# Bfloat16 partition sums and float32r parts for two batches of attention scores

## The chip, the cores and the metric

The kernel runs on one core of one Trainium2 chip. A core has a matrix engine (TensorE, PE in the profile), a vector engine (VectorE, DVE), a scalar engine (ScalarE, ACT), a general engine (GpSimd, POOL) and a queue engine that issues the transfers (SyncE, SP). The metric is the device time of one execution in microseconds.

## The reference, cut to what matters

Attention with a threshold on the scores, then an MLP with a residual (the "moe" part), then a mixing block (the "moe2" part). Four batches, eight heads, 576 tokens, 64 columns a head, 512 columns in all.

```python
scores = scale * np.matmul(q, k.transpose(0, 1, 3, 2))
thresh = np.max(scores, axis=-1, keepdims=True) - tau
scores = np.where(scores >= thresh, scores, -1000000000.0)
attn = np.exp(scores - np.max(scores, axis=-1, keepdims=True))
x = np.matmul(attn / (np.sum(attn, axis=-1, keepdims=True) + 1e-09), v)
...
xn = (x - mu) / np.sqrt(var + 1e-06) * g_ln
x = x + np.maximum(xn @ w_ch1, 0.0) @ w_ch2
...
theta = x @ w_theta
u = x + w_tok_r @ (x * np.cos(theta)) + w_tok_i @ (x * np.sin(theta))
out = u + np.maximum(u @ w_ch, 0.0)
```

## The kernel before

The program is written out by a planner (class Plan, lines 118 to 271). Each step of the work is an op with a function that issues its instructions, the ops that it depends on, the buffer places that it takes and gives back (Slot and Res), and an estimated cost on each engine that may run it. The planner plays these costs through eight times and then issues the instructions of every engine in the order of the best play. On the chip each engine works its list in that fixed order and waits where something isn't ready. PE's ops run in the order of a key: attention first, the MLP behind it. Where the play leaves PE without work for over 200 ns, `keep` (line 456) puts small filler matmuls.

Attention goes by couples: `couple(b, t, hp)` is one tile of 128 queries for two heads (pair hp) of batch b. There are four full tiles and one tail tile a batch (64 queries, the two heads stacked in one unit of 128 rows), and four pairs, so 16 full and 4 tail couples for each batch. `Keys` loads the transposed keys of a pair (tile kf, 128 x 576, line 753) and prepares its values; `Queries` loads one tile of queries for all four pairs (qf, line 855). `qk` (line 880) multiplies them in float32: two halves of 288 columns for each unit, where the two heads of a full couple stand on different rows of the array. `unit` then works on each unit: `top` (line 988, DVE) evicts and finds the maximum, `mask` and `expo` follow on ACT, `hi16` and `lo16` split P into two float16 parts (tile ringP), and a transposing DMA writes P's transposes (tile PT, line 1057; NPT places of the resource rPT). Batch 0 (WHOLE) uses transposes on PE instead, with PT as a float32 tile. `pv` (line 918) multiplies P and V into rows of x, for which it needs a free row tile (rXs, eight places). Nine row tiles serve two batches.

When three row tiles are complete, `ln_group` normalises them (tiles xn, resource rN, two places; the weight conversion `cvt` takes its tile a from the same two), makes the transposed operand ringX, and runs part A of the MLP: 12 of 16 chunks with `mlp1` (line 709, p_A) and `mlp2` (line 732, chA). There are six such groups. In groups (1,0) and (1,1) (LNQ) the transposition goes by DMA from a float16 tile x16 (resource rX16, two places); the others transpose on PE (line 1196). After attention, part B runs the other four chunks (p_B and c), then the mixing block follows (th, y, o).

Weights are loaded as raw words (tiles raw, resource rR, four places) and converted to two float16 parts. `group4` (line 566) converts four pieces with one common scale; for it, squares are summed over the partitions by a float32 matmul of one column with a matrix of ones (m5, line 607). It runs 13 times (eight for the MLP's weights, three for wtok, one each for wth and wch). `Keys.total` (line 796) does the same for the values of a pair in batches 1 to 3, 12 times, and `scales` (line 1492) for x, with nine such matmuls, twice. `one16` is a bfloat16 matrix of ones that the filler matmuls use already.

Of the kernel before, what the change touches and what calls it, by code (L numbers as in the profile page):

```python
# [22 lines left out]
KB = 4  # L23
# [9 lines left out]
NP16 = 4  # L33
NPT = 6
NRAW = 4
# [45 lines left out]
BUSY = 0.7  # L81
LATE = 25000.0
PVW = (2, 3)
XQ = (0, 1, 2)
# [190 lines left out]
def tile_kernel(  # L275
# [19 lines left out]
    def f(ap):  # L295
        return ap.bitcast(F32)

    def copy(e, out, in_):
        if e is A:
            A.activation(out=out, in_=in_, func=AF.Copy)  # L300
        elif e is V:
            V.tensor_copy(out=out, in_=in_)
        else:
            G.tensor_scalar(out=out, in0=in_, scalar1=1.0, scalar2=0.0, op0=ALU.mult, op1=ALU.add)  # L304
# [52 lines left out]
    rN = Res("xn", 2)  # L357
    rX16 = Res("x16", NX16)
    rG = Res("g", 8)
# [206 lines left out]
    def group4(name, pieces, acq, start, prev, kind, base, i, by_g, early=False):  # L566
# [38 lines left out]
        def m5(e):  # L605
            st["ps"] = m_tile(ms, [128, 512], f"pw_{name}")
            T.matmul(st["ps"][:, 0:1], lhsT=ones, rhs=st["q"][:, 4:5], start=True, stop=True)

# [132 lines left out]
    class Keys:  # L741


        def __init__(self, b, hp, prev):
# [6 lines left out]
            def load_f(e):  # L751
                k["f"] = ap.tile([128, 576], F32, tag=str(self.sk), name="kf_" + nm)
                Q.dma_start(k["f"], kT[b, hp, :, 0:576])


            self.ready = [op(load_f, prev, (self.sk,), Q=1100, kind=kd)]
            st = self.st = {}
# [38 lines left out]
            def total(e):  # L796
                st["ps"] = m_tile(ms, [128, 512], "pvs_" + nm)
                T.matmul(st["ps"][:, 0:1], lhsT=ones, rhs=st["vm"], start=True, stop=True)

# [43 lines left out]
    class Queries:  # L843


        def __init__(self, b, t, prev):
            nm = f"{b}_{t}"
            kd = "att" if not queries else "prep"
            self.sl = Slot(rQ, 4)
            c0 = 512 if t == TAIL else 128 * (t - 5 if b % 2 else t)  # L850
            q = self.q = {}

            def load_f(e):
                q["f"] = ap.tile([128, 4, 128], F32, tag=str(self.sl), name="qf_" + nm)
                Q.dma_start(q["f"], qT[b, :, :, c0:c0 + 128].rearrange("h p c -> p h c"))

            self.ready = [op(load_f, prev, (self.sl,), Q=1000, kind=kd)]

    def couple(b, t, hp):
# [20 lines left out]
        def qk(ws):  # L880
            def go(e):
                for w in ws:
                    w["S"] = psS.tile([128, 2, 512], F32, tag=str(w["ss"]), name="S_" + w["nm"])
                for n in range(2):
                    for w in ws:
                        r = slice(0, 128) if last else slice(64 * w["j"], 64 * w["j"] + 64)
                        T.matmul(w["S"][:, n, 0:288], lhsT=qd.q["f"][r, hp], rhs=d.k["f"][r, n * 288:(n + 1) * 288],  # L887
                                 start=True, stop=True)
            return go
# [3 lines left out]
        o_qk = qk_last[0] = op(qk(us), d.ready + qd.ready + [qk_last[0]], [w["ss"] for w in us],  # L893
                               (qd.sl,) + ((d.sk,) if final else ()), T=QKT if last else QKC, kind="att", **kw)
        for w in us:
# [221 lines left out]
    def ln_group(p, gi, base):  # L1117
# [44 lines left out]
        for t in range(nt):  # L1162
# [11 lines left out]

            s16 = Slot(rX16)

            def parts(t=t, s16=s16):
                if ("x16", t) not in st:
                    st["x16", t] = ap.tile([128, KB, 2, 128], F16, tag=str(s16), name=f"xn16_{nm}_{t}")
                return st["x16", t]  # L1180
# [311 lines left out]
    def scales(p):  # L1492
        ms, st = Slot(rM), {}

        def m(e):
            st["ps"] = m_tile(ms, [128, 512], f"px_{p}")
            for t in range(9):
                T.matmul(st["ps"][:, 0:1], lhsT=ones, rhs=cst(100 + 9 * p + t), start=(t == 0), stop=(t == 8))

# [18 lines left out]
        kw = dict(kind="ev")  # L1518
        o = op(m, sqs[p], (ms,), T=540, key=-1e6, **kw)
        sx_ops[p] = o = pow2(lambda: st["ps"][:, 0:1], lambda: px(p, X_S), 2.0 ** -30, [o], ms, "ev")  # L1520
# [493 lines left out]
```

## Time and profile before

| what | us |
| --- | --- |
| median of 3 runs | 820.85 (820.68 to 821.62) |
| profiled execution, its own time | 821.73 |
| its span | 819.95 |
| PE busy | 811.4 |
| DVE, ACT, POOL busy | 622.7, 531.7, 371.2 |

The span runs from the first to the last instruction of the profiled execution; the 1.78 us between it and the execution's own time lie outside the program. A row of the timeline gives the start of the first of several equal instructions, the time from there to the end of the last, the engine, the line, the operation with output and inputs, and their number after the x. A float32 matmul shows as two records. A matmul's time includes its way through the pipeline, so the distance from one start to the next says what it holds of the engine.

### The profile page before, as it was taken

The numbers are of one execution on the slowest core, as the hardware profiler recorded it, in microseconds if no ns is written. First come the engines' busy times: TensorE is split into PE (matmuls) and PEld (weight loads), VectorE is DVE, ScalarE is ACT, GpSimd is POOL, SyncE is SP. The second block draws the span as 40 slices with busy tenths as digits, with TensorE's granted clock in tenths as the row PEclk, the third lists the DMA queues.
The fourth block names the chain that finished last, engine by engine and source line by source line (L and its number), as shares of the span: only waits on it lengthen the run. The fifth ranks groups of instructions, "written<-read, shape, count | busy, mean of one in ns | idle before, by whom it ended". The sixth has DMA issues, their size and how long they took to land.

```text
span 819.9 us, 16404 instructions
## 1 busy us (share of the span) xinstructions
PE 811.4 (99%) x6145; PEld 533.8 (65%) x6145; DVE 622.7 (76%) x1291; ACT 531.7 (65%) x966; POOL 371.2 (45%) x462
## 2 busy tenths in 40 slices
PE   9999999999999999999999999999999999999997
PEld 8888866655566666656555555555545777567775
DVE  4879799999688788878757766666667886698843
ACT  4899999998678887887635444455466462474612
POOL 1332478688276468667612212212224470455611
PEclk9999999999999999999999999999999999999999
DMA  8334599996378898996971431663374105010011
GB/s 225 126 108 135 178 217 153 203 200 137 86 144 191 160 215 154 159 195 129 164 227 60 153 130 35 226 224 129 92 166 130 36 16 110 1 60 1 15 44 59
DMA packets 194351, 106.39 MB, mean 130 GB/s; under 512 B 157408, under 2 KB 175328, under 8 KB 194272
## 3 DMA queue, kind: packets, MB, share of 16 engines
q1 hardware_dynamic: 193984, 105.34, 53.7%
q8 instruction: 48, 0.79, 0.4%
q14 instruction: 31, 0.25, 0.1%
q10 hardware_dynamic: 288, 0.00, 0.0%
HBM read 52.50 MB, written 15.73 MB: 83 GB/s over the span
## 4 chain that ended last, share of the span: by engine, by line
PE 95%; ACT 2%; DVE 1%; issue 1%; POOL 0%; DVEq 0%; ACTq 0%; POOLq 0%
PE chA L732 17%; PE p_A L709 17%; PE y L1829 13%; PE S L887 11%; PE p_B L709 6%; PE c L732 6%; PE th L1665 5%; PE pv L902 5%; PE o L1887 4%; PE pv L915 4%; PE tm L965 2%; PE pv L910 2%; PE warm L454 1%; PE th_t L1665 1%; PE ptr L1196 1%
## 5 line engine op out<-in xcount | busy, mean ns | idle before, releaser
L709 PEld LDWEIGHTS <-w 128*128 128x128 f16 x1152 | 110.3, 98 | 80.3 <-issue 7.3
L709 PE MATMUL p_A<-ringX,w 128*128 128x384 f16 x864 | 149.8, 326 | 0.0
L732 PE MATMUL chA<-w,hbuf 128*128 128x512 f16 x648 | 149.4, 379 | 0.0
L732 PEld LDWEIGHTS <-hbuf 128*128 128x128 f16 x864 | 82.3, 99 | 93.7 <-issue 5.4
L994 DVE TENSOR_SCALAR_CACHE_REDUCE ringE<-S,ncoef 128x576 f32<-128x576 f32 x144 | 113.0, 812 | 25.1 <-PE S L887 20.5
L313 POOL TENSOR_TENSOR ringP<-ringE,ringP 128x512 f16<-128x512 f32 (+2 forms) x113 | 110.6, 992 | 18.0 <-ACT ringP L300 14.8
L1010 ACT ACTIVATE ringE<-ringE,tiny 128x576 f32<-128x576 f32 x144 | 105.5, 769 | 2.1 <-POOL tiny L1002 0.4
L887 PE MATMUL S<-kf,qf 64*128 64x288 f32 (+1 forms) x576 | 98.2, 426 | 0.0
L1829 PE MATMUL y<-tok,z 128*128 128x288 f16 x768 | 97.2, 286 | 0.0
L1829 PEld LDWEIGHTS <-z 128*128 128x128 f16 x768 | 75.1, 98 | 19.3
L1036 ACT ACTIVATE ringE<-ringE,ntaup 128x576 f32<-128x576 f32 x108 | 78.4, 764 | 0.1
L715 ACT ACTIVATE hbuf<-p_A 128x384 f16<-128x384 f32 x72 | 35.1, 488 | 57.0 <-PE p_A L709 56.5
L887 PEld LDWEIGHTS S<-kf,qf 64*128 64x128 f32 (+1 forms) x576 | 56.7, 186 | 21.8 <-issue 5.9
L1254 DVE SCALAR_TENSOR_TENSOR x<-chA,qs,x 128x512 f32<-128x512 f32 x54 | 40.3, 748 | 27.3 <-PE chA L732 27.1
L304 POOL TENSOR_SCALAR ringP<-ringE 128x576 f16<-128x576 f32 x59 | 42.6, 725 | 37.0 <-ACT ringE L1036 34.3
L718 DVE SCALAR_TENSOR_TENSOR hbuf<-p_A,hbuf 128x384 f16<-128x384 f32 x72 | 39.5, 550 | 17.1 <-ACT hbuf L715 16.6
L732 PE MATMUL c<-w,hbuf 128*128 128x512 f16 x216 | 50.8, 379 | 0.0
L709 PE MATMUL p_B<-ringX,w 128*128 128x384 f16 x288 | 50.6, 326 | 0.0
L1887 PE MATMUL o<-x1T,cw 128*128 128x288 f16 x384 | 47.7, 286 | 0.0
L313 DVE TENSOR_TENSOR ringP<-ringE,ringP 128x512 f16<-128x512 f32 (+2 forms) x55 | 44.6, 819 | 3.4 <-ACT ringP L300 2.8
L1887 PEld LDWEIGHTS <-cw 128*128 128x128 f16 x384 | 37.6, 98 | 9.7
L308 ACT ACTIVATE x1T<-u,cs 128x576 f16<-128x576 f32 x16 | 12.3, 770 | 47.7 <-DVE u L1856 41.9
(233 smaller groups left out, 1455.0 us busy)
## 6 DMA issues: line engine op xcount, KB each, us to landing
raw_w<-in_w SPq DMA_DIRECT2D x20, 512.0 KB, 4.6
rawe<-in_w SPq DMA_DIRECT2D x12, 512.0 KB, 4.8
raw_tok<-in_wtok SPq DMA_DIRECT2D x12, 432.0 KB, 3.9
qf<-in_qT SPq DMA_DIRECT2D x20, 256.0 KB, 3.3
kf<-in_kT SPq DMA_DIRECT2D x16, 288.0 KB, 3.7
xscr<-x SPq DMA_DIRECT2D x18, 256.0 KB, 2.5
xl<-xscr SPq DMA_DIRECT2D x18, 256.0 KB, 5.1
out<-uo SPq DMA_DIRECT2D x16, 288.0 KB, 2.1
```

What stands on the lines that cost most here:

```text
L304: G.tensor_scalar(out=out, in0=in_, scalar1=1.0, scalar2=0.0, op0=ALU.mult, op1=ALU.add)
L313: e.tensor_tensor(out=out, in0=a, in1=b, op=ALU.subtract)
L709: T.matmul(st["ps"][:, :n], lhsT=ch.w1(a, c), rhs=xt()[:, c, bb, :n], start=(kk == 0), stop=(kk == 11))
L732: T.matmul(ps, lhsT=h[:, a, t * 128:(t + 1) * 128], rhs=ch.w2(bb), start=(first and (a, bb) == M2[0]), stop=(stop and (a, bb) == M2[2]))
L887: T.matmul(w["S"][:, n, 0:288], lhsT=qd.q["f"][r, hp], rhs=d.k["f"][r, n * 288:(n + 1) * 288], start=True, stop=True)
L902: T.matmul(out[:, j * 65:j * 65 + 65], lhsT=(w["pt"] if t < 4 else cp["pt"])[:, c0:c0 + cs.stop - cs.start], rhs=d.st["raw"][:, t, j * 65: ...
L994: V.tensor_scalar(out=st["e"].rearrange("p (a k) -> p a k", a=2), in0=st["S"][:, :, 0:288], scalar1=ncoef, scalar2=None, op0=ALU.mult, op1 ...
L1010: A.activation(out=st["e"], in_=st["e"], func=AF.Prelu, bias=cp["thr"][:, j:j + 1], scale=-1.0, alpha=STEEP)
L1036: A.activation(out=e_of(ws), in_=e_of(ws), func=AF.Exp, bias=ntaup, scale=1.0)
L1665: T.matmul(st["ps"], lhsT=src(a, c), rhs=w[:, c * 512:(c + 1) * 512], start=(kk == 0), stop=(kk == 11))
L1829: T.matmul(st["ps"][n][:, 0:288], lhsT=a, rhs=w[:, n * 288:(n + 1) * 288], start=(k == 0 and q == 0), stop=(k == 8 and q == 2))
L1887: T.matmul(st["ps"][n][:, 0:288], lhsT=w[:, cs], rhs=d["t"][a][:, kk, n * 288:(n + 1) * 288], start=(kk == 0 and q == 0), stop=(kk == 3 an ...
```

## The change

Five edits are made together.

1. The sums over partitions (m5, `total`, and m in `scales`) take the upper 16 bits of the float32 number as bfloat16 and multiply with the bfloat16 ones. In `scales`, a DVE reduction (p0) first adds the nine columns, and one matmul stands for nine.
2. In batches 2 and 3 (those not in QF) keys and queries are loaded into a raw tile of the resource rN, copied to a float32r part hi, and the rest is subtracted into a float32r part lo. `qk` then makes three products in float32r (lo hi, hi lo, hi hi) in place of one in float32. The planner's costs of a couple are 1020 and 850 ns there (1230 and 1000 before).
3. P's transposes have five places in place of six.
4. LN's float16 rows of groups (1,0) and (1,1) take places of rR, those of the raw weights, and the resource rX16 is gone.
5. The constants follow.

```diff
--- before.py
+++ after.py
@@ -31,7 +31,7 @@
 NM = 4
 NE = 4
 NP16 = 4
-NPT = 6
+NPT = 5
 NRAW = 4
 WARM = 20
 WHOLE = ((0, 0), (0, 1), (0, 2), (0, 3))
@@ -80,6 +80,8 @@
 LNQ = ((1, 0), (1, 1))
 BUSY = 0.7
 LATE = 25000.0
+QF = (0, 1)
+QRC, QRT = 1020.0, 850.0
 PVW = (2, 3)
 XQ = (0, 1, 2)
 CX = [0, 760.0, 1250.0]
@@ -295,6 +297,9 @@
     def f(ap):
         return ap.bitcast(F32)
 
+    def top16(ap):
+        return ap.bitcast(BF16)[:, 1:2]
+
     def copy(e, out, in_):
         if e is A:
             A.activation(out=out, in_=in_, func=AF.Copy)
@@ -355,7 +360,6 @@
     rY = Res("y", 0)
     rXs = Res("x", NXS)
     rN = Res("xn", 2)
-    rX16 = Res("x16", NX16)
     rG = Res("g", 8)
     rR = Res("raw", NRAW)
     rQ, rK = Res("q", NQ), Res("k", NK)
@@ -604,7 +608,7 @@
 
         def m5(e):
             st["ps"] = m_tile(ms, [128, 512], f"pw_{name}")
-            T.matmul(st["ps"][:, 0:1], lhsT=ones, rhs=st["q"][:, 4:5], start=True, stop=True)
+            T.matmul(st["ps"][:, 0:1], lhsT=one16[:, 0:128], rhs=top16(st["q"][:, 4:5]), start=True, stop=True)
 
         def m9(e):
             V.tensor_scalar(out=base()[:, 8:12], in0=gsb, scalar1=s_(), scalar2=None, op0=ALU.mult)
@@ -752,8 +756,26 @@
                 k["f"] = ap.tile([128, 576], F32, tag=str(self.sk), name="kf_" + nm)
                 Q.dma_start(k["f"], kT[b, hp, :, 0:576])
 
-
-            self.ready = [op(load_f, prev, (self.sk,), Q=1100, kind=kd)]
+            sraw = Slot(rN)
+
+            def load_k(e):
+                k["raw"] = lp.tile([128, S], F32, tag=str(sraw), name="kraw_" + nm)
+                Q.dma_start(k["raw"], kT[b, hp, :, 0:576])
+
+            def hi_k(e):
+                k["hi"] = ap.tile([128, 576], F32R, tag=str(self.sk), name="khi_" + nm)
+                copy(e, k["hi"], k["raw"])
+
+            def lo_k(e):
+                k["lo"] = ap.tile([128, 576], F32R, tag=f"{self.sk}lo", name="klo_" + nm)
+                sub(e, k["lo"], k["raw"], f(k["hi"]))
+
+            if b in QF:
+                self.ready = [op(load_f, prev, (self.sk,), Q=1100, kind=kd)]
+            else:
+                o = op(load_k, prev, (self.sk, sraw), Q=1100, kind=kd)
+                o = op(hi_k, [o], A=ac(576), V=vc(576, .95), kind=kd)
+                self.ready = [op(lo_k, [o], (), (sraw,), G=gc(576), V=vc(576, 1.4), kind=kd)]
             st = self.st = {}
             src = v[b, hp].rearrange("(j p) c -> p j c", p=128)
             self.sc = None
@@ -795,7 +817,7 @@
 
             def total(e):
                 st["ps"] = m_tile(ms, [128, 512], "pvs_" + nm)
-                T.matmul(st["ps"][:, 0:1], lhsT=ones, rhs=st["vm"], start=True, stop=True)
+                T.matmul(st["ps"][:, 0:1], lhsT=one16[:, 0:128], rhs=top16(st["vm"]), start=True, stop=True)
 
             def s1(e):
                 V.tensor_scalar(out=st["s0"], in0=st["ps"][:, 0:1], scalar1=1.0e-36, scalar2=2.0 ** -28,
@@ -854,7 +876,26 @@
                 q["f"] = ap.tile([128, 4, 128], F32, tag=str(self.sl), name="qf_" + nm)
                 Q.dma_start(q["f"], qT[b, :, :, c0:c0 + 128].rearrange("h p c -> p h c"))
 
-            self.ready = [op(load_f, prev, (self.sl,), Q=1000, kind=kd)]
+            sraw = Slot(rN)
+
+            def load_q(e):
+                q["raw"] = lp.tile([128, S], F32, tag=str(sraw), name="qraw_" + nm)[:, 0:512].rearrange("p (h c) -> p h c", h=4)
+                Q.dma_start(q["raw"], qT[b, :, :, c0:c0 + 128].rearrange("h p c -> p h c"))
+
+            def hi_q(e):
+                q["hi"] = ap.tile([128, 4, 128], F32R, tag=str(self.sl), name="qhi_" + nm)
+                copy(e, q["hi"], q["raw"])
+
+            def lo_q(e):
+                q["lo"] = ap.tile([128, 4, 128], F32R, tag=f"{self.sl}lo", name="qlo_" + nm)
+                sub(e, q["lo"], q["raw"], f(q["hi"]))
+
+            if b in QF:
+                self.ready = [op(load_f, prev, (self.sl,), Q=1000, kind=kd)]
+            else:
+                o = op(load_q, prev, (self.sl, sraw), Q=1000, kind=kd)
+                o = op(hi_q, [o], A=ac(512), V=vc(512, .95), kind=kd)
+                self.ready = [op(lo_q, [o], (), (sraw,), G=gc(512), V=vc(512, 1.4), kind=kd)]
 
     def couple(b, t, hp):
 
@@ -881,17 +922,19 @@
             def go(e):
                 for w in ws:
                     w["S"] = psS.tile([128, 2, 512], F32, tag=str(w["ss"]), name="S_" + w["nm"])
-                for n in range(2):
-                    for w in ws:
-                        r = slice(0, 128) if last else slice(64 * w["j"], 64 * w["j"] + 64)
-                        T.matmul(w["S"][:, n, 0:288], lhsT=qd.q["f"][r, hp], rhs=d.k["f"][r, n * 288:(n + 1) * 288],
-                                 start=True, stop=True)
+                seq = (("f", "f"),) if b in QF else (("lo", "hi"), ("hi", "lo"), ("hi", "hi"))
+                for k, (a, c) in enumerate(seq):
+                    for n in range(2):
+                        for w in ws:
+                            r = slice(0, 128) if last else slice(64 * w["j"], 64 * w["j"] + 64)
+                            T.matmul(w["S"][:, n, 0:288], lhsT=qd.q[a][r, hp], rhs=d.k[c][r, n * 288:(n + 1) * 288],
+                                     start=(k == 0), stop=(k == len(seq) - 1))
             return go
 
         final = t == (8 if odd else TAIL)
         pts = []
         o_qk = qk_last[0] = op(qk(us), d.ready + qd.ready + [qk_last[0]], [w["ss"] for w in us],
-                               (qd.sl,) + ((d.sk,) if final else ()), T=QKT if last else QKC, kind="att", **kw)
+                               (qd.sl,) + ((d.sk,) if final else ()), T=(QKT if last else QKC) if b in QF else QRT if last else QRC, kind="att", **kw)
         for w in us:
             pts = pts + (unit(w, us, o_qk, d, whole, pen0, kw, cp, spv, sx_ if w is us[0] else ()) or [])
 
@@ -1172,11 +1215,12 @@
                     V.tensor_scalar(out=st["xn", t], in0=x[p, t0 + t], scalar1=rs[:, 0, t:t + 1],
                                     scalar2=rs[:, 1, t:t + 1], op0=ALU.mult, op1=ALU.add)
 
-            s16 = Slot(rX16)
+            s16 = Slot(rR)
 
             def parts(t=t, s16=s16):
                 if ("x16", t) not in st:
-                    st["x16", t] = ap.tile([128, KB, 2, 128], F16, tag=str(s16), name=f"xn16_{nm}_{t}")
+                    st["x16", t] = raw_tile(s16, f"xn16_{nm}_{t}").bitcast(F16).rearrange("p k two -> p (k two)")[:, 0:1024].rearrange(
+                        "p (c a k) -> p c a k", c=KB, a=2)
                 return st["x16", t]
 
             def hi_t(e, t=t, parts=parts):
@@ -1494,8 +1538,11 @@
 
         def m(e):
             st["ps"] = m_tile(ms, [128, 512], f"px_{p}")
-            for t in range(9):
-                T.matmul(st["ps"][:, 0:1], lhsT=ones, rhs=cst(100 + 9 * p + t), start=(t == 0), stop=(t == 8))
+            T.matmul(st["ps"][:, 0:1], lhsT=one16[:, 0:128], rhs=top16(st["sum"]), start=True, stop=True)
+
+        def p0(e):
+            st["sum"] = tiny(1)
+            V.tensor_reduce(out=st["sum"], in_=cst(100 + 9 * p, 9), op=ALU.add, axis=mybir.AxisListType.X)
 
         def p1(e):
             V.tensor_scalar(out=px(p, X_F, 3), in0=cst(C_R, 3), scalar1=px(p, X_S), scalar2=None, op0=ALU.mult)
@@ -1516,7 +1563,7 @@
             V.tensor_scalar(out=px(p, X_A), in0=cst(C_ISC), scalar1=px(p, X_R + 1), scalar2=None, op0=ALU.mult)
 
         kw = dict(kind="ev")
-        o = op(m, sqs[p], (ms,), T=540, key=-1e6, **kw)
+        o = op(m, [op(p0, sqs[p], V=150, **kw)], (ms,), T=60, key=-1e6, **kw)
         sx_ops[p] = o = pow2(lambda: st["ps"][:, 0:1], lambda: px(p, X_S), 2.0 ** -30, [o], ms, "ev")
         a = op(p1, [o, o_r], V=150, **kw)
         o = op(p3, [op(p2, [o, o_sth, o_k], V=150, **kw)], V=190, **kw)
```

## Rows read from the trace of the kernel before

**Rows 1.** Page, busy time: us, share of the span, instructions of each engine.

```profile
PE 811.4 (99%) x6145; PEld 533.8 (65%) x6145; DVE 622.7 (76%) x1291; ACT 531.7 (65%) x966; POOL 371.2 (45%) x462
```

**Rows 2.** Page, the chain that ended last: shares of the span by engine.

```profile
PE 95%; ACT 2%; DVE 1%; issue 1%; POOL 0%; DVEq 0%; ACTq 0%; POOLq 0%
```

**Rows 3.** Windows of 50 and 200 us: length, busy time of each engine, clock, DMA.

```profile
150.00:200.00 50.00, 49.04 (x446) 29.47 (x445) 49.40 (x106) 46.33 (x86) 38.23 (x43) 1.00 0.98 192
200.00:400.00 200.00, 200.00 (x1688) 123.29 (x1686) 159.84 (x362) 156.52 (x266) 128.21 (x174) 1.00 0.81 156
```

**Rows 4.** Timeline, PE, a full couple of batch 2: start us, us, instructions merged.

```profile
231.62 0.98 PE L915 MATMUL pv<-va,PT 128*128 128x130 f16 x18
232.54 1.24 PE L887 MATMUL S<-kf,qf 64*128 64x288 f32 x8
233.71 0.66 PE L709 MATMUL p_A<-ringX,w 128*128 128x384 f16 x3
```

**Rows 5.** Timeline, PE, two tail couples of batch 2 and what follows.

```profile
302.63 2.10 PE L887 MATMUL S<-kf,qf 128*128 128x288 f32 x8
304.57 1.46 PE L732 MATMUL chA<-w,hbuf 128*128 128x512 f16 x6
```

**Rows 6.** Timeline, PE, mix stage: float16 matmuls of 288 columns.

```profile
642.67 6.04 PE L1829 MATMUL y<-tok,z 128*128 128x288 f16 x48
648.55 0.90 PE L1829 MATMUL y<-tok,hbuf 128*128 128x288 f16 x6
```

**Rows 7.** Timeline, PE, batch 0: float32 PV of 65 columns.

```profile
57.14 1.00 PE L902 MATMUL pv<-vraw,PT 128*128 128x65 f32 x8
57.98 0.39 PE L902 MATMUL pv<-vraw,ringP 128*128 128x65 f32 x2
```

**Rows 8.** Timeline, PE, batch 1: float16 PV of 65 columns.

```profile
131.10 1.01 PE L910 MATMUL pv<-va,PT 128*128 128x65 f16 x28
132.03 1.24 PE L887 MATMUL S<-kf,qf 64*128 64x288 f32 x8
```

**Rows 9.** Timeline, PE: sums over partitions, each with the row after it.

```profile
551.54 0.28 PE L607 MATMUL pw_tok<-tiny,ones 128*128 128x1 f32 x2
551.68 0.81 PE L732 MATMUL c<-w,hbuf 128*128 128x512 f16 x3
...
222.33 0.36 PE L798 MATMUL pvs<-tiny,ones 128*128 128x1 f32 x2
222.55 0.81 PE L732 MATMUL chA<-w,hbuf 128*128 128x512 f16 x3
...
583.60 2.06 PE L1498 MATMUL px<-cs,ones 128*128 128x1 f32 x18
```

**Rows 10.** Lines by form: copy and subtractions; busy us, mean ns, idle before.

```profile
L300 ACT ACTIVATE ringP<-ringE 128x576 f16<-128x576 f32 x47 | 31.5, 673 | 1.9 <-DMA PT<-ringP 1.7
L313 POOL TENSOR_TENSOR ringP<-ringE,ringP 128x512 f16<-128x512 f32 x75 | 89.2, 1193 | 8.7 <-ACT ringP L300 5.9 <-DMA PT<-ringP 1.3
L313 DVE TENSOR_TENSOR ringP<-ringE,ringP 128x512 f16<-128x512 f32 x33 | 26.5, 804 | 2.9 <-ACT ringP L300 2.8
```

**Rows 11.** Page, DMA issues: KB each, us from issue to landing.

```profile
kf<-in_kT SPq DMA_DIRECT2D x16, 288.0 KB, 3.7
```

**Rows 12.** Timeline around 190 to 220 us: SP's transposes of P, PE's PV.

```profile
188.97 9.04 SPq L1057 DMA_TRANSPOSE PT<-ringP  x4
...
219.80 2.70 PE L910 MATMUL pv<-va,PT 128*128 128x65 f16 x84
```

**Rows 13.** Windows, instructions on the tile raw_w alone, 200 to 390 us.

```profile
200.00:390.00 190.00, 0.00 (x0) 0.00 (x0) 0.00 (x0) 1.00 0.79 155
```

**Rows 14.** Windows of line 732; timeline of SP and PE, 250 to 260 us.

```profile
250.00:258.00 8.00, 5.36 (x23) 2.05 (x24) 1.00 1.17 256
...
252.12 0.34 SPq L1221 DMA_DIRECT2D scr<-ringX  x1
...
258.33 1.95 PE L709 MATMUL p_A<-ringX,w 128*128 128x384 f16 x11
```

## Prediction

> **What bounds the kernel now.** I read the busy table first: TensorE (PE) is busy for 811.4 of 819.9 us [rows 1]. Matmuls are pipelined and a busy PE need not be a full one, so I read the chain of work that ended last next: 95% of it is PE's own instructions, one after the other [rows 2]. Then the windows by stage, for the two stages that the change meets. From 200 to 400 us, where batches 2 and 3 are scored, PE has 200.0 us of 200 while VectorE (DVE) has 159.8, ScalarE (ACT) 156.5 and GpSimd (POOL) 128.2; from 150 to 200 us, the end of batch 1, DVE has 49.4 of 50 [rows 3]. The MLP of part A is what keeps PE full there: whenever a couple of heads isn't ready, an MLP matmul is. So a microsecond taken from PE's own work is a microsecond of the end, as long as there is MLP work left to put in its place; a delay of another engine costs only where that supply runs out. I therefore price PE by the distance between starts in its timeline, not by the durations, which include the drain.
>
> **Scores of batches 2 and 3.** A full couple (two heads on two halves of the rows) is eight float32 records, and the next matmul starts 1.17 us after the first [rows 4]. A tail couple (one unit over all 128 rows) is four; two of them take 1.94 us, so 0.97 each, 0.2425 a record [rows 5]. A float16 matmul of the same 288 columns takes 5.88 / 48 = 0.1225 us [rows 6]. One float32 product of 288 columns is two records, 0.485, that is four of those. In a full couple the two halves run side by side: four pairs at 0.2425 are 0.97, and 0.20 is entry and exit. The change makes three products where there was one: six pairs for a full couple, six single matmuls for a tail. No row shows a float32r matmul. Bounds from the nearest rows: 0.1225 a pair if it streams like float16, 0.2425 if like a float32 record. I take 0.1225: the four-to-one ratio says that float32 is made of single passes, and a product of two rounded parts should need one. Then both kinds go from 0.97 to 6 x 0.1225 = 0.735, entry and exit unchanged: 0.235 saved, 40 times (32 full, 8 tail couples): 9.4 us. By the upper bound it is 6 x 0.2425 - 0.97 = 0.485 lost, 40 times: 19.4 us.
>
> The Trainium skill ("FP8 and Floating Point Precision", TensorE Precision Notes) has true float32 as four passes, and a reduced form that truncates to 22 bits; the first half agrees with the 0.485 against 0.1225, the second no row here shows.
>
> **The loads of weights.** Each of the six pairs needs its weights loaded. The nearest price is the float32 PV of batch 0, where 65 columns don't cover the load: eight records in 0.84 us, 0.105 each [rows 7]. That is under 0.1225, so it hides if it may run beside the matmul before it. In the tail couple it does: the records follow at 0.2425, twice 0.1225 with no room for 0.105 more, all in the same rows of the array [rows 5, 6]. I take it as hidden; the other end is in the rivals.
>
> **Partition sums.** These have one column each; 13 in group4, 12 in Keys.total. One holds PE between 0.14 us and 0.22 us from its start to the next matmul's [rows 9], as two float32 records. In bfloat16 it is one short matmul; the nearest is the 65-column float16 PV at 0.93 / 28 = 0.033 us [rows 8]. Saved 0.11 to 0.19, 25 times: 2.8 to 4.8, I take 3.7. The two sums of scales are nine float32 matmuls each, 18 records in 2.06 us [rows 9] of which 1.93 is pitch (0.107 x 18); they become one. Saved 1.9 each, 3.8. The added reduction p0 is one small DVE instruction ahead of the sum, priced at 0.15 us by the plan and never in PE's way: PE has part B's matmuls on both sides there. Rounding of the sum costs no time.
>
> **The added preparation.** Eight key tiles and ten query tiles now land in a raw tile, are copied to hi (ACT or DVE) and subtracted into lo (POOL or DVE). Nearest rows: the 576-wide copy on ACT 0.673, the 512-wide subtraction 1.193 on POOL and 0.804 on DVE [rows 10]. Some 18 x 0.7 + 18 x 1.1 = 32 us, over three engines that leave 155 us of 600 free from 200 to 400 us [rows 3]: hidden beside PE. The loads keep their place on SP's queue; the matrix then waits for load, copy and subtraction, 3.7 [rows 11] + 0.7 + 1.2 and two hops. Queued behind that are only QK and what follows it on PE's list; PE does MLP meanwhile. The raw tiles share two places with LN's xn and the weight conversion, so several loads in a row go two at a time. Where this cover is gone (batch 2's first keys come before 200 us, beside a DVE at 49.4 of 50) four keys and two queries, 6 x 1.8 = 11 us of side work, push batch 1's end back. If LN's 16-bit rows had to wait for raw weights they would be late, but no conversion works in these places from 200 to 390 us [rows 13]: nothing.
>
> **Five places for P's transposes.** Six transposes of batch 1's last tile are issued by 198.0 us (two earlier, then the four from 188.97 on), and PV takes the pile up only at 219.80 [rows 12], when a row tile of x comes free from part A. With five, the sixth is transposed after the first PV, and what follows comes one or two transposes later, some 2 us. Who waits: the last couple of batch 1, and through it LN of group (0,2). Group (0,2)'s operand is complete when its spill is issued at 252.12, and its first matmul is at 258.33: 6.2 us of margin, in which PE has its last 23 chA matmuls of the groups before [rows 14]. PE reaches this point sooner by 14 sums (2.1 us) and eight couples (1.9 us): 4.0. With 2 us for the places the margin is just used up. I charge 1.5 us for a wait here and for the three sums in batch 0, where PE isn't short of time.
>
> **Sum.** 9.4 + 3.7 + 3.8 - 1.5 = 15.4 us. The profiled execution is 821.73 us with a span of 819.95; 15.4 off is 806.3, and the median of the runs is 0.9 below that execution: 805.5 us.
>
> **Rivals.** (1) The loads aren't hidden. Each pair then costs 0.1225 + 0.105 = 0.2275, six 1.365, 0.395 more than now: 15.8 us lost on 40 couples, 7.5 won on the sums, 1.5 for the wait: about 831 us, slower. It decides from a pair of 0.19 us on, where 40 x (6 x 0.19 - 0.97) eats the 7.5. Against it: the tail records [rows 5, 6]. The Trainium skill ("TensorE: Matmul & The Clock Gate", Part 3) lets a load overlap a running matmul only where the row group differs; the tail couples' trace doesn't bear that out, by the same rows. Chance 0.04. (2) float32r streams like a float32 record: 19.4 lost, 7.5 won, 834 us. Chance 0.06. (3) The supply of MLP work runs out around 250 us: the preparation of batch 2 falls on the full DVE and five places hold back the last couple, so that LN of (0,2) comes 5 to 8 us late. For it: the margin of 6.2 and DVE's 49.4; against it: a PE that is sooner also frees x's rows sooner. Gain 7.5 to 12: 809 to 813, say 811 us. Chance 0.16. (4) The change doesn't shorten the attention stage at all, because the freed time on PE fills with waits of the pipeline of heads; left are the sums after 440 us (two of scales, seven of group4, 4.9 us): 816 us. Against it: the MLP supply, and the chain [rows 2]. Chance 0.08.
>
> **How the numbers follow.** Forecast 0.66, between 801 and 809: 0.5 us for the sums, 1.5 for the tail couples' pitch, and 3 for the new order of all engines' lists, since one changed price moves them all. With (3) this makes 0.82: the range is 801 to 813. A measurement of this kernel can tell about 0.2% from no change, 1.6 us. Faster: forecast, (3) and (4), 0.90; slower: (1) and (2), less a case between, 0.09; within 0.2%: 0.01.
>
> **What would show it.** The score matmuls of batches 2 and 3 as 12 records of a full couple with the next matmul about 0.93 us after the first (1.17 before), and 0.735 for a tail; a pitch of 0.2275 or 0.2425 would be rivals 1 and 2. The sums as single records of some 0.03 us, and one px where 18 records stood. PE still busy for all of 200 to 400 us, with 40 couples' time less; an idle stretch of PE near 245 to 260 us, ended by LN, would be rival 3. What would make it wrong without a rival: filler matmuls or waits of more than 4 us in the first 100 us, where nothing stands in for PE.

## The result and the profile after

| what | before | after |
| --- | --- | --- |
| median, us (range of 4 runs each) | 821.08 (820.68 to 821.62) | 808.49 (807.9 to 809.48) |
| profiled execution, its span | 821.73, 819.95 | 808.34, 806.2 |
| PE, DVE, ACT, POOL busy | 811.4, 622.7, 531.7, 371.2 | 798.3, 634.5, 533.6, 395.2 |

The ratio is 0.9847 with an interval of 0.983 to 0.9865: 12.6 us faster, where the sum of the forecast was 15.4 (805.5 us) with a range of 801 to 813. It lies 0.5 us inside the upper end of the narrower forecast of 801 to 809.

Busy time and the chain that ended last, from the page of the kernel after. They answer to [rows 1] and [rows 2]: PE is still busy for 99% of the span, and the other engines carry more than before. The chain is less purely PE's (92%, before 95%).

```profile
PE 798.3 (99%) x6243; PEld 529.7 (66%) x6243; DVE 634.5 (79%) x1305; ACT 533.6 (66%) x980; POOL 395.2 (49%) x470
...
PE 92%; ACT 3%; DVE 2%; issue 1%; DMA 1%; POOL 0%; DVEq 0%; POOLq 0%
```

Windows of the kernel after (length, busy time of PE, PEld, DVE, ACT, POOL, clock, DMA share, GB/s), which answer to [rows 3]. The stage of batches 2 and 3 is as full as it was, 199.80 of 200 us, though it now holds 1849 matmuls in place of 1688.

```profile
150.00:200.00 50.00, 49.61 (x454) 30.57 (x453) 48.75 (x111) 44.27 (x83) 40.92 (x44) 1.00 0.80 151
200.00:400.00 200.00, 199.80 (x1849) 129.57 (x1848) 168.70 (x365) 159.37 (x279) 138.40 (x174) 1.00 0.84 161
```

Timeline of PE in the kernel after (start, us from there to the last end, line, operation, number merged): a full couple of batch 2, then two tail couples, one behind the other (the last product of the first isn't shown). They answer to [rows 4] and [rows 5].

```profile
228.59 0.54 PE L930 MATMUL S<-khi,qlo 64*128 64x288 f32 x4
228.97 0.42 PE L930 MATMUL S<-klo,qhi 64*128 64x288 f32 x4
229.23 0.42 PE L930 MATMUL S<-khi,qhi 64*128 64x288 f32 x4
229.58 0.66 PE L713 MATMUL p_A<-ringX,w 128*128 128x384 f16 x3
...
299.37 1.47 PE L736 MATMUL chA<-w,hbuf 128*128 128x512 f16 x6
300.49 0.61 PE L930 MATMUL S<-khi,qlo 128*128 128x288 f32 x2
300.94 0.42 PE L930 MATMUL S<-klo,qhi 128*128 128x288 f32 x2
...
301.46 0.42 PE L930 MATMUL S<-khi,qlo 128*128 128x288 f32 x2
301.72 0.42 PE L930 MATMUL S<-klo,qhi 128*128 128x288 f32 x2
301.99 0.43 PE L930 MATMUL S<-khi,qhi 128*128 128x288 f32 x2
302.25 0.52 PE L958 MATMUL pv<-va,PT 128*128 128x130 f16 x7
```

Read the starts, not the durations. In the full couple the second product starts 0.38 us after the first, the third 0.26 after that, the next matmul 0.35 later: 0.99 in all, where the float32 couple took 1.17. Two pairs in 0.26 are 0.13 a pair (the median over the couples of batches 2 and 3 is 0.1305); entry and exit keep about 0.2. In the second tail couple six matmuls take 302.25 - 301.46 = 0.79, so 0.132 each, where four float32 records took 0.97. Each of them has its own load of weights, on the same rows of the array as the matmul before it, and there is no room in 0.132 for a load of 0.105: the loads are hidden.

This is the only one of the eight tail couples that shows 0.79; the others show 0.88 to 1.02 (median of all 0.93). Behind MLP work most of that is a matter of where the profile puts the start: the six chA matmuls ahead of the first tail couple hold 1.12 in place of 6 x 0.216 = 1.30, its first product 0.45 in place of 0.26, and the two together are what their pitches give. In the two tail couples behind PV it is a loss: the first matmul holds 0.22 and 0.24 there.

Timeline of PE after: a sum over the values of a pair and one of x's scales, each with the row behind it. They answer to [rows 9].

```profile
235.80 0.17 PE L820 MATMUL pvs<-tiny,one 128*128 128x1 bf16 x1
235.82 1.46 PE L713 MATMUL p_A<-ringX,w 128*128 128x384 f16 x8
...
618.88 0.17 PE L1541 MATMUL px<-tiny,one 128*128 128x1 bf16 x1
618.91 1.46 PE L1712 MATMUL th<-th,x1T 128*128 128x512 f16 x6
```

Of the 25 small sums 20 hold PE for 0.025 to 0.029 us, two for 0.04 and three for 0.10 (mean 0.037). Before they held it for 0.14 to 0.31 (mean 0.18), and the nine-column sum of the scales for 1.93; the 2.06 of its row includes the way through the pipeline.

A ledger of PE shows where the 13.75 us of the span went. For every matmul the time to the next start is added up by its output, in both traces; waits fall to the operation ahead of them:

| PE's time by output, us | before | after | difference |
| --- | --- | --- | --- |
| S, full couples | 76.24 | 70.89 | -5.35 |
| S, tail couples | 15.62 | 15.19 | -0.43 |
| p_A and chA, the MLP work among the couples | 284.54 | 283.70 | -0.84 |
| pw and pvs (25 small sums) | 4.61 | 0.92 | -3.69 |
| px (two sums of scales) | 3.85 | 0.06 | -3.80 |
| warm: fillers (39 before, 52 after) | 4.80 | 6.40 | +1.61 |
| warm: float32 matmuls of the start | 7.14 | 6.01 | -1.13 |

The scores with the MLP work among them are 6.6 us, the sums 7.5, the fillers take 1.6 back: 12.5. Nearly all of the MLP work's 0.84 belongs to the tail couples: it is the early start told of above. The float32 matmuls of the start are the same 40 in both kernels and took between 5.9 and 7.5 us in the profiles of this case, so their 1.13 is not put down to the change. The two profiled executions differ by 13.4 us, the medians by 12.6. The waits of PE in the kernel after are few (engine, line, what it waited for: us, times, longest), and none lies between 245 and 260 us:

```profile
PE pvs L820 <- ACT va L813: 1.3, 2, 1.1
PE warm L458 <- POOL ones L424: 1.0, 1, 1.0
PE pw_w L611 <- ACT tiny L605: 0.3, 1, 0.3
PE pt L1664 <- DVE r_t L1730: 0.2, 1, 0.2
```

### The profile page after: what moved, and what is told of

It reads as the page before. It is cut to its first block, busy times and chain, and to the rows that moved or that the text cites. A ratio compares the mean times of both kernels' runs of the same rounds, so it can differ in the third digit from the quotient of the medians.

```text
span 806.2 us, 16608 instructions
## 1 busy us (share of the span) xinstructions
PE 798.3 (99%) x6243; PEld 529.7 (66%) x6243; DVE 634.5 (79%) x1305; ACT 533.6 (66%) x980; POOL 395.2 (49%) x470
## 4 chain that ended last, share of the span: by engine, by line
PE 92%; ACT 3%; DVE 2%; issue 1%; DMA 1%; POOL 0%; DVEq 0%; POOLq 0%
PE p_A L713 17%; PE chA L736 16%; PE y L1876 13%; PE S L930 9%; PE p_B L713 6%; PE c L736 6%; PE th L1712 5%; PE o L1934 5%; PE pv L945 4%; PE pv L958 4%; PE tm L1008 2%; PE pv L953 2%; PE warm L458 1%; DMA vraw<-in_v 1%; PE th_t L1712 1%
## 5 line engine op out<-in xcount | busy, mean ns | idle before, releaser
L318 POOL TENSOR_TENSOR ringP<-ringE,ringP 128x512 f16<-128x512 f32 (+2 forms) x118 | 123.0, 1056 | 13.5 <-ACT ringP L305 8.6
L309 POOL TENSOR_SCALAR ringP<-ringE 128x576 f16<-128x576 f32 x64 | 47.7, 748 | 41.1 <-ACT ringE L1079 39.3
L930 PE MATMUL S<-kf,qf 64*128 64x288 f32 (+1 forms) x288 | 50.0, 426 | 0.1
L1712 PE MATMUL th<-th,x1T 128*128 128x512 f16 x192 | 42.6, 379 | 0.0
L528 POOL TENSOR_TENSOR raw_w<-raw_w 128x512 int32<-128x512 int32 x20 | 21.3, 1068 | 41.4 <-DVE raw_w L523 16.8
```

Of the source, the lines that this page charges most:

```text
L318: e.tensor_tensor(out=out, in0=a, in1=b, op=ALU.subtract)
L930: T.matmul(w["S"][:, n, 0:288], lhsT=qd.q[a][r, hp], rhs=d.k[c][r, n * 288:(n + 1) * 288], start=(k == 0), stop=(k == len(seq) - 1))
L1712: T.matmul(st["ps"], lhsT=src(a, c), rhs=w[:, c * 512:(c + 1) * 512], start=(kk == 0), stop=(kk == 11))
```

## The experiments

The first question was how the two gains divide, the second whether PE is what bounds, the third whether the added preparation is hidden, the fourth what the order of the engines' lists does. Ratios are to runs of the kernel before on the same chip (medians 821.46 to 821.76); a difference to the kernel after is one of medians, and the runs of before moved by 0.7 us between chips.

**The sums alone.** The kernel before with only the bfloat16 sums:

```diff
-            T.matmul(st["ps"][:, 0:1], lhsT=ones, rhs=st["q"][:, 4:5], start=True, stop=True)
+            T.matmul(st["ps"][:, 0:1], lhsT=one16[:, 0:128], rhs=top16(st["q"][:, 4:5]), start=True, stop=True)
 (and so in total and in scales, with p0)
```

> The kernel before with the bfloat16 sums alone (group4, Keys.total and scales), six places for P's transposes, float32 scores everywhere. Theory A (PE's own time is the end, wherever it is taken): the 25 sums give 3.7 us and the two of scales 3.8 us, 7.5 us in all, so 813.5 us against 821.0. Theory B (in the attention stage freed PE time is lost in waits, only what lies behind it counts): 4.9 us, 816 us.

Measured: 817.02 us, ratio 0.9943 (0.9931 to 0.9956), so 4.4 us, less than either theory. The ledger gives the sums 7.36 us, nearly as in the kernel after (7.48). The rest went into three more fillers (0.6), longer couples in batch 1 (1.1), the MLP work (0.6) and a wait of PE that neither whole kernel has (of the waits of this kernel):

```profile
PE o L1893 <- DVE x1T L1868: 0.7, 1, 0.7
```

The sums are worth what was forecast on PE, and three fifths of it arrives.

**The parts alone.** The kernel after with the three sums in float32 again:

```diff
-            T.matmul(st["ps"][:, 0:1], lhsT=one16[:, 0:128], rhs=top16(st["q"][:, 4:5]), start=True, stop=True)
+            T.matmul(st["ps"][:, 0:1], lhsT=ones, rhs=st["q"][:, 4:5], start=True, stop=True)
 (and so in total and in scales, without p0)
```

> The changed kernel with the float32 sums put back: float32r parts, five places and LN's rows in the raw weights' places alone. Theory A: the pitch measured in the changed kernel (0.1305 a pair, 0.1325 a tail matmul, against the 0.97 of a float32 couple) gives 32 x 0.187 + 8 x 0.175 = 7.4 us less, 813.6 us. Theory B (a part of it is given back in waits that the five places or the preparation make): 4 to 5.5 us less, 815.5 to 817 us.

Measured: 819.31 us, ratio 0.9971 (0.9961 to 0.9982), so 2.2 us, again less than either theory. On PE the scores gain 6.6, as in the kernel after. It stands 10.8 us behind the kernel after, which is the 7.5 of the sums and 3.3 of new waits: y 1.4 (two waits between 636.9 and 639.5 us), p_A 1.2 at 197.2, and 0.7 ahead of tm. Of the waits view of this kernel:

```profile
PE p_A L713 <- DVE w L539: 0.9, 1, 0.9
...
PE y L1873 <- POOL z L318: 0.6, 1, 0.6
```

Alone the two halves give 4.4 and 2.2, 6.6 together, but 12.6 when made together. So the halves don't add up: about half of the gain of the whole depends on which order the planner writes.

**Five places alone.** The kernel before with NPT = 5.

```diff
-NPT = 6
+NPT = 5
```

> The kernel before with five places for P's transposes in place of six, nothing else. Theory A (PE has MLP work whenever attention is held back): within 0.5 us of the kernel before. Theory B (the fifth place holds back the last couple before LN of group (0,2), as the prediction charged): 1 to 2 us slower, with a PE wait near 250 us.

Measured: 822.80 us, ratio 1.0017 (1.0008 to 1.0026), 1.3 us slower, the loss of theory B without its wait: no wait of PE stands near 250 us. Instead there are 52 fillers where 39 stood, and 0.9 us of waits of S at 170 to 171. The fillers, by tile (three durations in ns, from and to us), of the kernel before and then of this one:

```profile
L462 PE MATMUL warm<-one x39: 272/273/284, 8.1 to 161.9; 128*128 128x256 bf16 x39
```

```profile
L462 PE MATMUL warm<-one x52: 272/273/284, 7.6 to 164.2; 128*128 128x256 bf16 x52
```

A filler holds PE for 0.123 us (6.40 / 52). Thirteen more are 1.6, in the part of the kernel where PE has no MLP work to put in; the kernel after shows the same number, between 7.0 and 162.7 us.

**Six places in the kernel after.** The one edit undone (the small tiles' room is cut to make space):

```diff
-NPT = 5
+NPT = 6
-NTINY = 960
+NTINY = 820
```

> The changed kernel with six places for P's transposes again; room for the sixth is made by a smaller tile of small numbers (820 of 960 columns, the rest unused). Theory A (the fifth place's loss is real, 13 more filler matmuls on PE in the first 160 us, as in the run with five places alone): 79 to 82 filler records in place of 92 and 1.3 to 1.6 us less, 807 us. Theory B (five places cost only by the order that they happened to give): within 1 us of 808.5 either way.

Measured: 817.95 us, ratio 0.9957 (0.9944 to 0.9971): 9.5 us slower than the kernel after, although it has ten fillers fewer (42); neither theory had that. Timeline of PE in the mix stage, with the idle time ahead of a row and its releaser in brackets, and windows of the same stretch:

```profile
627.76 3.84 PE L1876 MATMUL y<-tok,z 128*128 128x288 f16 x30
632.97 0.66 PE L1876 MATMUL y<-tok,z 128*128 128x288 f16 x4 [1.37 <-ACT z L305]
634.84 2.10 PE L1876 MATMUL y<-tok,z 128*128 128x288 f16 x8 [1.21 <-POOL z L318]
```

```profile
632.00:634.00 2.00, 0.66 (x4) 0.31 (x4) 2.00 (x3) 0.91 (x2) 2.00 (x2) 1.00 0.29 72
634.00:636.00 2.00, 1.16 (x5) 0.74 (x6) 1.95 (x3) 0.00 (x0) 0.78 (x1) 0.53 0.16 59
...
638.00:640.00 2.00, 2.00 (x10) 1.20 (x9) 1.94 (x5) 1.78 (x3) 0.98 (x2) 0.50 0.04 8
640.00:642.00 2.00, 2.00 (x14) 1.42 (x13) 2.00 (x5) 1.43 (x3) 1.34 (x2) 0.77 0.00 0
```

PE stood still for 2.6 us waiting for z, and then ran at a granted clock of 0.50 (1.2 GHz in place of 2.4) until past 640 us; the two together cost y 6.0 us. One of its six runs kept a mean granted clock of 1.000 and still took 816.27, so the clock is the smaller part of the 9.5. S waited 1.8 us, 1.6 of them at 200 to 203 us. A stage that has nothing to do with P's transposes thus became slower: the order of all lists changed. What the sixth place itself is worth in the kernel after can't be separated from that.

**float32r in batch 1 as well.**

```diff
-QF = (0, 1)
+QF = (0,)
```

> The changed kernel with float32r parts for batch 1 as well (batches 1 to 3), batch 0 in float32. Theory A: 16 full couples at 0.187 and 4 tail couples at 0.17 are 3.7 us more, 804.8 us. Theory B (between 100 and 200 us DVE at 49 of 50 is the bound, and the parts of batch 1 are more work for it): no gain, or up to 3 us slower than the changed kernel.

Measured: 823.19 us, ratio 1.0022 (1.0013 to 1.0031), 14.7 us behind the kernel after, far more than theory B allowed. The scores themselves gained another 3.8 us on PE. The window of the kernel after to compare, then window and waits of this kernel:

```profile
90.00:180.00 90.00, 88.65 (x888) 58.46 (x887) 85.61 (x188) 85.15 (x162) 67.74 (x85) 1.00 0.86 186
```

```profile
90.00:180.00 90.00, 79.25 (x854) 56.36 (x852) 86.27 (x190) 76.16 (x144) 65.40 (x71) 0.98 0.71 158
```

```profile
PE pw_w L611 <- ACT tiny L605: 4.9, 2, 3.4
```

PE loses 9.4 us in this window alone, and the fillers are 102 in place of 52. In batch 1 DVE is near full in both kernels (85.6 and 86.3 of 90) and MLP work is scarce. That the preparation is what delays PE is argued from this and not shown: no wait of PE names a key's or a query's part. The longest are those of a weight's sum for its small tile from ACT, and the order of the lists is another one here too.

**Two products in place of three.** lo(q) times hi(k) is left out of the scores of batches 2 and 3.

```diff
-                seq = (("f", "f"),) if b in QF else (("lo", "hi"), ("hi", "lo"), ("hi", "hi"))
+                seq = (("f", "f"),) if b in QF else (("hi", "lo"), ("hi", "hi"))
```

> The changed kernel with two products instead of three: the one of q's lo with k's hi is left out. Theory A (from 200 us on PE's own work is the end): two pairs of 0.1305 for 32 couples and two matmuls of 0.1325 for 8, 10.5 us less, 798 us. Theory B (in the attention stage freed PE time goes into waits of the other engines): less than half of it, 803 to 808 us.

Measured: 798.02 us, ratio 0.9713 (0.97 to 0.9725), 10.5 us below the kernel after. Two pairs less in each of 40 couples are 40 x 2 x 0.131 = 10.5. This is theory A. The planner's costs are unchanged, and so is the order of every engine's list; the waits of PE are those of the kernel after (the longest 1.1 in both). The window:

```profile
200.00:400.00 200.00, 200.00 (x1783) 125.26 (x1781) 176.77 (x384) 167.18 (x292) 143.84 (x183) 1.00 0.88 169
```

With nothing but PE's own work changed, a microsecond of PE was a microsecond of the end. This is the fastest of all kernels here, with one product left out.

**The preparation three times, in the same order.** Every copy and subtraction of hi and lo is issued three times; the planner's costs stay, so the lists keep their order.

```diff
-                copy(e, k["hi"], k["raw"])
+                for _ in range(3):
+                    copy(e, k["hi"], k["raw"])
 (and so for lo and for the queries)
```

> The changed kernel with each copy to hi and each subtraction to lo of keys and queries issued three times in a row; the planner's costs are left as they are, so the lists of all engines keep their order. About 64 us more work on ACT, DVE and POOL together. Theory A (the preparation hides beside PE's MLP work): within 1 us of 808.5. Theory B (the preparation is on the path where DVE is full, batch 2's keys at 190 to 210 us, and explains the missing 3 us of the forecast): 4 us or more slower, with PE waiting there.

Measured: 835.07 us, ratio 1.0156 (1.0142 to 1.0171), 26.6 us behind the kernel after, as theory B had it. Window and waits:

```profile
200.00:400.00 200.00, 184.94 (x1633) 118.38 (x1632) 171.57 (x352) 160.68 (x280) 132.08 (x165) 0.98 0.74 146
```

```profile
PE S L934 <- DVE klo L318: 4.1, 3, 2.1
PE S L934 <- POOL klo L318: 3.2, 1, 3.2
```

PE is idle for 15 us of 200, and the longest of its waits are score matmuls that wait for klo (7.3 us) and, behind them, for qlo (2.9). They stand near 209 and 218 us, close to where theory B put them, and again at 325, 338 and 355 us. No MLP matmul steps in: PE's list is fixed, and what stands behind a late score waits with it.

**The preparation three times, planned as such.** The same instructions, with the planner's costs of these steps three times as high too.

```diff
-                o = op(hi_k, [o], A=ac(576), V=vc(576, .95), kind=kd)
+                o = op(hi_k, [o], A=3 * ac(576), V=3 * vc(576, .95), kind=kd)
 (and so for lo and for the queries)
```

> Every copy to hi and subtraction to lo three times, as in the earlier run, but now the planner's costs of these ops are three times as high, so that the lists are ordered for it. Theory A (the 835 us came from PE's fixed list: a score matmul that comes late holds all that stands behind it): most of the 26.6 us is gone, 809 to 818 us. Theory B (64 us of side work more than the engines can take): 825 us or more again.

Measured: 830.84 us, ratio 1.0105 (1.0068 to 1.0142), so theory B.

```profile
200.00:400.00 200.00, 190.41 (x1650) 121.63 (x1650) 175.53 (x352) 155.72 (x267) 132.44 (x163) 0.97 0.70 139
```

```profile
PE S L934 <- DVE qlo L318: 3.1, 1, 3.1
PE pv L962 <- DVE hbuf L722: 2.8, 2, 2.1
```

A planner that knows of the load gets back 4.2 us of 26.6, give or take 3, and no more. The granted clock has a part in it: the four runs of this kernel took 826.38, 828.97, 832.71 and 833.34 us at mean granted clocks of 0.999, 0.996, 0.992 and 0.990, and the window is from the last of them. The side engines have spare time on the average (DVE 175.5 of 200), but three times the work is hidden by it in neither of the two orders. How much the single preparation costs is not measured by either run.

**Two products and no lo of the queries.** As above, and the subtraction that made lo(q) isn't issued.

```diff
-                o = op(hi_q, [o], A=ac(512), V=vc(512, .95), kind=kd)
-                self.ready = [op(lo_q, [o], (), (sraw,), G=gc(512), V=vc(512, 1.4), kind=kd)]
+                self.ready = [op(hi_q, [o], (), (sraw,), A=ac(512), V=vc(512, .95), kind=kd)]
```

> Two products as in the earlier run (q's lo with k's hi is left out), and q's lo isn't made: ten subtractions and their tiles less. Theory A (the preparation that the plan knows of is hidden): within 1.5 us of that run's 798.0. Theory B (it costs what stands on the full engines): 10 us of side work less give 2 us or more.

Measured: 803.58 us, ratio 0.9779 (0.9764 to 0.9793): 5.6 us slower than with lo(q) made and not used, which neither theory had. Every engine's list has another order here, already from the first batch on; that this costs the 5.6, and not the work that is gone, is argued. Its longest new wait of PE:

```profile
PE ptr L1239 <- DVE xn L1214: 2.2, 1, 2.2
```

On whether the preparation is hidden this says nothing; it is a further example of what the order does.

**Other prices, the same work.** The planner's cost of a couple, once upwards for a full one and downwards for a tail, once downwards for a full one. Both kernels do the work of the kernel after; only the order, the choice among engines and the fillers can differ.

```diff
-QRC, QRT = 1020.0, 850.0
+QRC, QRT = 1080.0, 805.0
```

> The changed kernel with one line changed: the planner's costs of the float32r couples are 1080 and 805 ns (as the trace has them) in place of 1020 and 850. The same instructions, another order. Theory A (the time is the sum of PE's instructions and the order hardly matters): within 1 us of the changed kernel, 808 us. Theory B (each new order has waits of its own of 0 to 10 us, and the changed kernel's is one without): 808 to 818 us, with PE waits that the changed kernel doesn't have.

```diff
-QRC, QRT = 1020.0, 850.0
+QRC, QRT = 960.0, 850.0
```

> As the run before, with 960 in place of 1020 and 850 left: a second order of the same instructions. Theory A: 808 us. Theory B: 808 to 818 us.

Measured: 818.55 us upwards, ratio 0.9958 (0.9943 to 0.9973); 813.98 downwards, ratio 0.9907 (0.9891 to 0.9924). Both have the waits of theory B; the first lies 0.6 us beyond its range. The first has 83 fillers in place of 52: with the waits behind them they take 5.4 us more than in the kernel after, and the scores 3.3 more. A wait of the first, then waits of the second:

```profile
PE ptr L1240 <- ACT xn L1212: 1.0, 1, 1.0
```

```profile
PE y L1876 <- ACT hbuf L305: 1.4, 1, 1.4
PE p_A L713 <- DVE w L539: 1.1, 1, 1.1
```

The same work takes 808.5, 814.0 or 818.6 us, by 45 to 60 ns in one or two prices. The kernel after is the lowest of the three. The prediction gave no reason to expect that of its order, so for the prediction it is luck.

**The pitch of float32r by itself.** Twelve unused float32r matmuls of each of six widths, all on 128 rows and with a load of the same weights each, ahead of the first sum of the scales; the small tiles' room is cut for their operand.

```diff
+                for n_ in (64, 128, 192, 288, 384, 512):
+                    for _ in range(12):
+                        T.matmul(st["ps"][:, 0:n_], lhsT=rnd[:, 0:128], rhs=rnd[:, 0:n_], start=True, stop=True)
```

> The changed kernel with 72 more float32r matmuls ahead of the first sum of scales: 12 each of 64, 128, 192, 288, 384 and 512 columns, 128 rows, weights loaded for each. The pitch tells why a pass of 288 columns took 0.1325 us and not the 0.1225 of float16. Theory A (a constant is added to each matmul with 4-byte weights): 0.173 for 384 and 0.226 for 512 columns, and a floor of some 0.11 to 0.13 for 64 and 128. Theory B (the load, 0.13 us, is the bound): 0.13 at every size to 288, then 0.1625 and 0.216 as in float16. Theory C (4-byte columns stream slower by 8%): 0.176 and 0.235.

The burst in PE's timeline of that kernel, and a row of float16 matmuls of 512 columns of the kernel after, with the row behind it:

```profile
576.95 10.74 PE L1545 MATMUL px<-rnd 128*128 128x64 f32 x72
587.54 0.18 PE L1546 MATMUL px<-tiny,one 128*128 128x1 bf16 x1
```

```profile
620.93 2.75 PE L1712 MATMUL th<-th,x1T 128*128 128x512 f16 x12
623.52 5.31 PE L1876 MATMUL y<-tok,z 128*128 128x288 f16 x42
```

| columns | 64 | 128 | 192 | 288 | 384 | 512 |
| --- | --- | --- | --- | --- | --- | --- |
| median us from start to start | 0.112 | 0.1115 | 0.111 | 0.131 | 0.173 | 0.231 |
| ns a column | | | | 0.455 | 0.451 | 0.451 |

Up to 192 columns nothing changes: there is a floor of 0.111 us. That it is the load of the weights is argued (each matmul has one), and no run has the matmuls without it. From 288 on the time goes with the columns, 0.45 ns each. So 384 and the floor are as in theory A, and 512 columns lie between A and C. Float16 has 2.59 / 12 = 0.216 for 512 columns, 0.42 ns each, and 0.1225 / 288 = 0.425 [rows 6]. So float32r streams 6 to 7% slower than float16 in one pass, and 288 columns lie just above the floor. (This kernel's own time, 821.19 in one run, has the burst and another order in it and is not used.)

## Why the prediction held, and where its steps failed

**PE bounds the stage: held.** PE stayed full from 200 to 400 us, and the run with two products turned 10.5 us less of PE's work into 10.5 us less of time.

**The loads are hidden, and one pass is enough: held.** Rivals 1 and 2 asked for a pitch of 0.2275 or 0.2425; it is 0.1305 in pairs and 0.132 in the tails. The float32 rows that the prediction took for this left more room than it said, as 0.1225 + 0.105 = 0.2275 lies under 0.2425 too; 0.132 leaves none. The Trainium skill ("TensorE: Matmul & The Clock Gate", LDWEIGHTS) gives a load as columns over 1.2 GHz, an estimate of 107 ns for 128 columns. The floor of 0.111 us in the burst agrees; float16 does not, for PV loads 128 columns for each matmul and its matmuls follow at 0.033 [rows 8]. The sentence of the Trainium skill that the prediction cites ("TensorE: Matmul & The Clock Gate", Part 3), by which a load runs beside a matmul only on other rows, does not agree with the tails: at 0.132 a matmul, on the same rows, there is no room for it.

**The size of the scores' term: too large, the main miss.** The step "I take 0.1225" for a pair, the pitch of float16, failed. A full couple now holds PE for 0.99 (median of the 32): 0.24 for the first pair with its entry, four at 0.13, and 0.225 from the last pair to the next matmul. That is 0.18 less than 1.17; six matmuls of 0.132 make a tail couple 0.175 shorter. 32 x 0.18 + 8 x 0.175 = 7.2 us in place of 9.4. (The expectation of the parts alone counted 0.187 for a full couple and so 7.4.) In the trace the couples of batches 2 and 3, with the MLP work's 0.84, are 7.0 shorter; the ledger's 6.6 holds, against that, 0.4 by which three couples of batch 1 became longer. That 288 columns cost more than float16's was within the bounds but not expected.

The Trainium skill ("FP8 and Floating Point Precision", TensorE Precision Notes) has true float32 as four passes and a reduced form that truncates; the 0.1305 beside 0.485 for a float32 product (two records of 0.2425) agrees with one pass against four, except for those 6 to 7%.

**The sums: held.** 3.7 + 3.8 forecast, 3.69 + 3.80 measured. The range of 0.14 to 0.22 for one sum was read from two; over all 25 it is 0.14 to 0.31, with a mean of 0.18, the middle of what was read.

**The charge of 1.5 us: near in size, wrong in mechanism.** It was to be a wait of PE for LN of group (0,2) near 250 us. There is none: the spill of its operand is issued at 250.80 (before at 252.12 [rows 14]), and its first matmul comes at 253.63. What came instead are 13 more fillers between 7 and 163 us, 1.6 us, the number that five places alone bring. That the size fits is luck. Rows of SP and PE in the kernel after:

```profile
195.86 0.60 SPq L763 DMA_DIRECT2D kraw<-in_kT  x1
198.91 7.10 SPq L763 DMA_DIRECT2D kraw<-in_kT  x3
...
250.80 0.35 SPq L1265 DMA_DIRECT2D scr<-ringX  x1
...
201.95 0.53 PE L930 MATMUL S<-khi,qlo 64*128 64x288 f32 x4
...
253.63 0.65 PE L713 MATMUL p_A<-ringX,w 128*128 128x384 f16 x3
```

The first keys of batch 2 are loaded only at 195.86 and three more from 198.91 on, spread over 7.1 us, and the first score of batch 2 starts at 201.95 (before at 192.7). So the preparation did come late at the one place that the prediction named, but nothing that sets the end waited for it. Rival 3 put a price on this that the run didn't charge.

**"PE does MLP meanwhile": wrong as an argument.** On the chip PE has a fixed list. MLP work covers a late key only if the planner put it ahead of that score; with the preparation three times as long PE was idle for 15 us. In the kernel after this cover holds, as no wait for klo or qlo shows, since the list happens to have enough work ahead of each score, not because PE chooses.

**Three microseconds for the order: too small.** With the same work two other prices gave 5.5 and 10 us more; either half of the change alone lost about 3 us to waits and fillers. That the forecast came near is in part luck: the kernel after is written in an order with few waits, and the same work in the two other orders, 814.0 and 818.6, lies above the range of 801 to 813. Why the planner's orders meet such waits isn't settled; the runs show where they stand (z ahead of y, the scale of a weight, xn ahead of its transposes, and up to 31 more fillers in the first 175 us), not which of its costs is wrong.

## What to carry to other kernels

Price a float32r product by its own pitch (0.131 us for 288 columns, 0.111 at the least in the burst here), not by float16's, and three of them, 0.39, still beat one float32 product, 0.485. Where a planner writes fixed lists, an edit's price on its engine and the price of the new order are two terms: take the second from runs in which only a price is changed, before a difference of 1% is put down to the edit. A supply of other work hides a late operand only as far as the list has it ahead of the waiting instruction.

## What the runs showed of the hardware

float32r costs 0.45 ns a column in place of float16's 0.42, and 0.111 us at least where each matmul has its own load of weights. A bfloat16 matmul of one column mostly holds PE for some 0.03 us between others, where the float32 one held it for 0.18 in the mean. In the kernel with six places PE waited for 1.37 and 1.21 us shortly after one another; its granted clock was at 0.53 and 0.50 from 634 to 640 us, and back at 1.00 from 642 on; waits and clock together cost 6.0 us. In other runs with 0.9 to 1.5 us of idle time there (parts alone, prices downwards) the clock of the 20 us stayed at 1.00.
